# Attention with a gated MLP on one core: one tile of each unit's exponentials folded on GpSimd instead of VectorE

## The chip, the core and the metric

The kernel runs on one core of one Trainium2 chip. The metric is the device time of one execution in microseconds; before the change the median of three runs is 1235.76 us (1235.67 to 1236.98). The engines are TensorE (PE in the profile), VectorE (DVE), ScalarE (ACT), GpSimd (POOL) and SyncE (SP), which here only issues DMAs. Each engine works through its own instructions in order and waits for other engines by semaphores.

## The reference

`x` is the layer norm of `A_x` (2048 tokens, width 512). Attention has 32 heads of width 128 against a cache of 2048 keys; beside it runs an MLP with shifted columns, and its result gates the attention's.

```
xn = layernorm(A_x)
q = xn @ wq                                    # 32 heads x 128
p = softmax(q @ k_cache^T / sqrt(128))         # 2048 x 2048 per head
s = (p @ v_cache) @ wo
hs = shift(gelu(layernorm(xn) @ w1)) @ w2      # four column blocks, shifted by 1, -1, 2, -2 tokens
x1 = xn + hs
g = silu(x1 + gelu(layernorm(x1) @ w3) @ w4)
out = A_x + s * g
```

## The kernel before

The program has a prologue (layer norms and the MLP, up to about 118 us), one long attention loop, and a tail with the last unit in halves.

**Units and slots.** Attention is cut into 128 units: a unit is one head for 512 queries. The order is by groups of four heads (`NG` = 8 groups), in a group by block of queries (`QT` = 4), in that by head. A unit has eight slots (`SPU`); slot p computes the scores of 256 keys against 512 queries on TensorE (`s_slot`, two matmuls of 512 columns into one PSUM tile) and their exponentials on ScalarE (line 436), which go to a tile `pT` of 128 x 4 x 512 in bf16. Two slots fill one such tile, so a unit has four: slots 0 and 1, 2 and 3, 4 and 5 (the third tile), 6 and 7. The ring holds six. `pv_slot` multiplies them by the values ten slots later (`LAG`).

The loop over `n = u * SPU + p` writes out all engines' order by hand: `pin` keeps every instruction in the order in which the program issues it. So an instruction of VectorE that waits holds up everything that stands behind it on VectorE.

**The softmax sums.** VectorE adds the unit's four tiles: `add_first` (line 442, tiles 0 and 1, at slot 4), `add_next(u, 2)` (line 447, third tile, at slot 6), and in slot 0 of the next unit `add_next(u, 3)` (line 447, fourth tile). Then `fold` (line 451) adds the upper half of the 2048 columns to the lower, and `fold_last` (line 455) does it once more, which leaves 128 x 512. SyncE issues a transposing DMA of that (`turn`, line 480, slot 3). In slot 0 of the unit after, `turned_sums` (line 485) sums the transposed tile `tT`, `turned_recip` (line 491) inverts it, and two DMAs (`dr`, line 493, and `rb`, line 497) spread it over the partitions. At slot 7 `norm` (line 509) multiplies the unit's output `ps_o` by it.

So slot 0 of unit u holds on VectorE, in this order: the column sum and the reciprocal of unit u - 2, the last add of unit u - 1; then come, mixed with parts of the query product, the two folds of unit u - 1.

**The query products.** From unit 16 on, the query projection of two heads at a time is computed in seven smaller products (`product`, on block sums of `x` and of the weights), started two units ahead. TensorE writes them into one PSUM tile (tag `xa`); `q_take` (ScalarE, line 405) and `q_part` (VectorE, lines 413, 416, 418, 421) combine them into the queries. Lines 416 and 418 stand around the fold of an odd unit's slot 1; product 4, at slot 4 of the odd unit, writes where they read, and so waits for line 418. In the profile it is the matmul `ps_q<-xnT,wc`. The block sums of the weights are made by `w_sum` (line 365), four small subtractions for every pair of heads, two per unit, at slots 2 and 6 of two units.

**The output.** Each unit also has one tile of 128 tokens of the output projection (`wo_mm`, four matmuls into `ps_wo`), added to the sums `sacc` at slot 7 (`wo_post`, line 571). In the last groups the gate is applied: for the later two blocks of queries in group 6 by a product into a temporary `tm` and an add (lines 564 and 567); for the earlier two in group 7 by line 580, and the residual by line 582. `tm` has two buffers in the pool `pS`. Also for the later blocks lines 537 and 542 scale the sums and add the residual, once per unit, in some of the units before that.

GpSimd has work in the prologue alone: an iota, some memsets, and the powers of the layer norms (lines 194 and 205).

Of the kernel before, what the change touches and what calls it, by code (L numbers as in the profile page):

```python
# [9 lines left out]
ALU = mybir.AluOpType  # L10
FP32 = mybir.dt.float32
BF16 = mybir.dt.bfloat16
# [5 lines left out]
def kernel(  # L18
# [15 lines left out]
    nc = tc.nc  # L34
    P = nc.NUM_PARTITIONS
# [15 lines left out]
    HG = 4  # L51
    NG = H // HG

    SPU = KC // 2
# [7 lines left out]
    pin = tc.keep_in_program_order  # L62
# [48 lines left out]
    def mm(out, lhsT, rhs, start, stop, **kw):  # L111
# [9 lines left out]
        out=ident[:], in0=diag[:], scalar1=0.0, scalar2=None, op0=ALU.is_equal))  # L121
# [9 lines left out]
    kTs, vBs, wqs, wos, oTs, st = {}, {}, {}, {}, {}, {}  # L131
    todo = defaultdict(list)

    def at(n, fn):
        todo[n].append(fn)
# [179 lines left out]
    def q_mm(u, dcs, tag="xa"):  # L315
        g, qt, hh = units[u]
        if dcs[0] == 0:
            st[u] = dict(psq=psX.tile([P, 512], FP32, tag=tag, name="ps_q"))
        for dc in dcs:
            mm(st[u]["psq"][:], wqs[g * HG + hh][:, dc, :],  # L320
               xnT[:, dc, qt * 512:(qt + 1) * 512], dc == 0, dc == DC - 1)
# [37 lines left out]
    def w_sum(h, i):  # L359
        if i == 0:  # L360
            wc[h] = pS.tile([P, 4, 2, Dh], BF16, tag="wc", bufs=2, name="wc")
        w, o = wc[h], [wc[h][:, k] for k in range(4)]
        b11, b12, b21, b22 = (wqs[h + j][:, d, :] for d in (LO, HI) for j in (0, 1))
        a, b = ((b12, b11), (b22, o[0]), (b22, b12), (b21, o[1]))[i]
        pin(nc.vector.tensor_tensor(out=o[i], in0=a, in1=b, op=ALU.subtract))
# [59 lines left out]
    def s_slot(u, p):  # L425
        g, qt, hh = units[u]
        s = st[u]
        sps = psS.tile([P, 2, 512], FP32, name="ps_s")
        for j in range(2):
            kc = 2 * p + j  # L430
            kv = kTs[g * HG + hh].rearrange("d (i p j) -> d i j p", p=P, j=KJ)
            mm(sps[:, j, :], kv[:, kc // KJ, kc % KJ, :], s["qT"], True, True)
        if p % 2 == 0:
            s.setdefault("pT", []).append(pB.tile([P, 4, 512], BF16, tag="pT", bufs=6, name="pT"))
        jj = 2 * (p % 2)
        pin(nc.scalar.activation(  # L436
            out=s["pT"][-1][:, jj:jj + 2, :], in_=sps[:], func=ACT.Exp, scale=SCALE))

    def add_first(u):
        s = st[u]  # L440
        s["acc"] = pB.tile([P, 4, 512], BF16, tag="acc", bufs=2, name="acc")
        pin(nc.vector.tensor_tensor(  # L442
            out=s["acc"][:], in0=s["pT"][0][:], in1=s["pT"][1][:], op=ALU.add))

    def add_next(u, i):
        a = st[u]["acc"]
        pin(nc.vector.tensor_tensor(out=a[:], in0=a[:], in1=st[u]["pT"][i][:], op=ALU.add))  # L447

    def fold(u):
        a = st[u]["acc"]  # L450
        pin(nc.vector.tensor_tensor(out=a[:, 0:2, :], in0=a[:, 0:2, :], in1=a[:, 2:4, :], op=ALU.add))  # L451

    def fold_last(u):
        a = st[u]["acc"]
        pin(nc.vector.tensor_tensor(out=a[:, 0, :], in0=a[:, 0, :], in1=a[:, 1, :], op=ALU.add))  # L455
# [22 lines left out]
    def turn(u):  # L478
        st[u]["tT"] = pB.tile([P, 4, P], BF16, tag="tT", bufs=2, name="tT")
        pin(nc.sync.dma_start_transpose(out=st[u]["tT"][:], in_=st[u]["acc"][:, 0, :]))  # L480

    def turned_sums(u):
        s = st[u]
        sm = s["sm"] = smp.tile([P, 4], FP32, name="sm")
        pin(nc.vector.tensor_reduce(out=sm[:], in_=s["tT"][:], axis=mybir.AxisListType.X, op=ALU.add))  # L485

    def turned_recip(u):
        s = st[u]
        sm = s["sm"]
        rc = smp.tile([P, 4], FP32, name="rc")  # L490
        pin(nc.vector.reciprocal(out=rc[:], in_=sm[:]))
        s["dr"] = drp.tile([P, 4], FP32, name="dr")
        pin(nc.sync.dma_start(out=s["dr"][:], in_=rc[:]))

    def bcast(u):
        st[u]["rb"] = pB.tile([P, 512], FP32, tag="rb", bufs=2, name="rb")
        pin(nc.sync.dma_start(
            out=st[u]["rb"][:], in_=st[u]["dr"][:].rearrange("p j -> (p j)").partition_broadcast(P)))
# [52 lines left out]
    def pay():  # L551
        while owed:
            y_out(*owed.popleft(), nc.sync)
# [280 lines left out]
    pS = None  # L834
    for h in range(HG):
        load_wo(h)
    for g in range(NG - 1):
        b = (g * QT + QT - 1) * HG
        for hh in range(HG):
            h = (g + 1) * HG + hh  # L840
# [30 lines left out]
    def pv_run(n):  # L871
        while pv_at[0] <= n - LAG:
            pv_slot(*divmod(pv_at[0], SPU))
            pv_at[0] += 1
# [9 lines left out]
    UA, UB = NU - 2, NU - 1  # L884

    def wo_slot(part, n, each=2, **kw):
        gg, t = wo_todo[0]
        if part < HG // each:
            wo_mm(gg, t, tuple(range(part * each, (part + 1) * each)), **kw)
            return  # L890
        wo_todo.popleft()
        wo_post(gg, t, n)
        if gg == NG - 1 and t % 4 < 3 and t + 1 not in fin and t // 4 not in LATE:
            fin_load(t + 1)

    FIRST, LAST = 16, NU - 4
    pairs = range(FIRST, LAST + 1, 2)
    q_plan = defaultdict(list)
    steps = defaultdict(list)
    first, third = {}, {}  # L900
    for v in pairs:
        a = (v - 2) * SPU
# [8 lines left out]
    def fold_at(u):  # L911
        return 1 if u in third else 0

    def run_steps(n, which):
        for fn, v, k in steps.get(n, ()):
            if fn is which:
                fn(v, k)
# [4 lines left out]
    for h in range(HG, H, 2):  # L922
        u = (h // HG) * QT * HG + (-4, -2)[h % HG // 2]
        for i in range(4):
            at((u + i // 2) * SPU + (2, 6)[i % 2], lambda h=h, i=i: w_sum(h, i))

    for v in range(1, NU):
        if v not in made and not FIRST <= v < LAST + 2:
# [3 lines left out]
    for n in range(UB * SPU):  # L932
        u, p = divmod(n, SPU)
        extra = len(wo_todo) > 1 and u in (2 * HG, 2 * HG + 1)
        if p == 0 and wo_box:
            wo_slot(4, n, each=1)
        s_slot(u, p)
        pv_run(n)
        for v, dcs in q_plan.get(n, ()):
            q_mm(v, dcs)  # L940
        run_steps(n, product)
        run_steps(n, q_take)
        if p == 0 and 1 <= u:
            if u - 2 in TURN:
                turned_sums(u - 2)
                turned_recip(u - 2)
            add_next(u - 1, 3)
        if p == 1 and u - 2 in TURN:
            bcast(u - 2)
        if p == fold_at(u) and 1 <= u:  # L950
            for v in third.get(u, ()):
                q_part(v, 1)
            fold(u - 1)
            for v in third.get(u, ()):
                q_part(v, 2)
            if u != UA and u not in first:
                fold_last(u - 1)
        if p == 2 and u in first:
            q_part(first[u], 0)
            fold_last(u - 1)  # L960
        if p == 3 and u - 1 in TURN:
            turn(u - 1)
        if p == 0:
            twice = extra
        if twice and p < 3:
            wo_slot(p, n, tag="xa")
        for v, k in ((u + 1, 3), (u + 2, 7)):
            if p == k and "psq" in st.get(v, ()) and (k == 3) == (v > FIRST):
                q_copy(v)
        if u - 2 in TURN:  # L970
            norm_p, sum_p, wo_p, each = 7, 5, 3, 1
        else:
            norm_p, sum_p, wo_p, each = 4, 5, 4, 1
        at_wo = [wo_p + i for i in range(HG // each + 1)]
        if FIRST - 2 <= u < LAST:
            at_wo = ([1, 3, 4, 6, 7], [0, 2, 3, 6, 7])[u % 2]
        if p == norm_p and 2 <= u and not u - 2 in TURN:
            norm_queue(u - 2)
        if p == sum_p and 1 <= u and u - 1 not in TURN:
            sums(u - 1)  # L980
        if p == sum_p + 1 and 1 <= u and u - 1 not in TURN:
            bcast(u - 1)
        if u == UA and p in (1, 2, 3):
            wo_slot(p - 1, n)
            if p == 3:
                fold_last(u - 1)
        if p in at_wo and wo_todo and pS is not None and (p == at_wo[0] or wo_box):
            wo_slot(at_wo.index(p), n, each=each)
        if p == norm_p and u - 2 in TURN:
            norm_queue(u - 2)  # L990
        run_steps(n, q_part)
        if p == 4:
            add_first(u)
        if p == 6:
            add_next(u, 2)
        pay()
        held_mm(n)
        for fn in todo.pop(n, ()):
            fn()
        if pS is None and not held:  # L1000
            right.close()
            pS = right.enter_context(pool("pS", side="right", reuse_waits="tile"))
# [31 lines left out]
    def pv_to(k):  # L1034
# [29 lines left out]
        out=diag[:], in0=diag[:], scalar1=0.0, scalar2=None, op0=ALU.is_equal))  # L1064
# [98 lines left out]
```

## Time and profile before

| | |
|---|---|
| median of three runs | 1235.76 us (1235.67 to 1236.98) |
| the profiled execution | 1236.42 us |
| its span, first to last instruction | 1234.6 us |
| scores, values, output projection, queries in the loop | from about 118 to 1213 us |
| exponentials, line 436 | 1016 of 1025 ns |
| line 447 (third and fourth tile) | 254 of 1208 ns |
| line 442 (first two tiles) | 127 of 1224 ns |
| transposes of the sums to landing | 2.6 / 3.6 / 6.0 us (least, median, most) |

Engine names in the profile: PE is the matmul, PEld its weight loads, and SPq stands for what SyncE's queue issues. A timeline row gives the start in us, the duration in us, engine, line, operation, output and inputs, their shapes, a count, and in brackets how long the engine had been idle and what ended it. Consecutive instructions of VectorE overlap by some 0.09 us, so that their starts lie closer than their durations. A matmul of 512 columns shows 0.38 us, but they follow one another every 0.216 us. A group's row gives the count, the busy time in us and the mean in ns of one, and the engine's idle time before them. A row of the windows gives the length, then for PE, PEld, DVE, ACT and POOL the busy time and the number of instructions, the granted clock of TensorE, the DMA engines' share and GB/s.

### The profile page before, as it was taken

The page shows a single profiled execution, that of the slowest core. Times are in us where ns is not written, and L with a number is a line of the kernel's source. Part 1 is how long each engine was busy: PE and PEld are TensorE (multiplying, and loading weights), DVE is VectorE, ACT ScalarE, POOL GpSimd, SP SyncE. Part 2 cuts the span into 40 slices and gives each one's busy share as a digit, 9 for nine tenths or more (in the row PEclk, how much of TensorE's full clock was granted, in tenths as well). Part 3 has the DMA queues.
Part 4 walks back from the last instruction along what each step waited for, and adds up shares of the span by engine and source line. Part 5 has one row for each costly group of instructions (what it writes and reads, how often), then busy time and mean ns, then how long its engine had stood idle before and what let it go on. Part 6 is the DMA issues. An engine that isn't in the chain of part 4 may idle for free.

```text
span 1234.6 us, 17534 instructions
## 1 busy us (share of the span) xinstructions
PE 1227.5 (99%) x6267; PEld 636.5 (52%) x6267; DVE 1030.1 (83%) x1647; ACT 1105.8 (90%) x1237; POOL 26.6 (2%) x75
## 2 busy tenths in 40 slices
PE   9999999999999999999999999999999999999998
PEld 6444444455555555555555555555555555555545
DVE  7712778899888888988889888888889999999997
ACT  6345999899999999999999999999999999999996
POOL 5300000000000000000000000000000000000000
PEclk9999999999999999999999999999999999999999
DMA  8661122664334423354243523543345424553342
GB/s 176 168 140 35 31 39 65 96 99 94 63 80 100 106 57 82 87 111 85 58 95 91 111 56 69 103 104 72 76 83 111 107 58 90 99 107 66 77 81 66
DMA packets 244056, 107.75 MB, mean 87 GB/s; under 512 B 194816, under 2 KB 227712, under 8 KB 243968
## 3 DMA queue, kind: packets, MB, share of 16 engines
q1 hardware_dynamic: 243408, 106.17, 41.5%
q8 instruction: 49, 0.80, 0.3%
q10 hardware_dynamic: 560, 0.46, 0.1%
q14 instruction: 39, 0.32, 0.1%
HBM read 67.50 MB, written 2.36 MB: 57 GB/s over the span
## 4 chain that ended last, share of the span: by engine, by line
PE 94%; DVE 3%; DMA 2%; ACT 1%; issue 0%; SPq 0%; DVEq 0%; ACTq 0%
PE ps_s L112 39%; PE ps_o L112 37%; PE ps_wo L112 8%; PE ps_q L112 8%; PE ps_m L112 2%; DMA tT<-acc 1%; DVE acc L447 1%; ACT pT L436 1%; DMA rb<-dr 0%; DMA xin<-in_A_x_dram 0%; DVE sm L485 0%; PE ps_oh L112 0%; DVE oT L509 0%; DVE acc L451 0%; DVE y L1025 0%
## 5 line engine op out<-in xcount | busy, mean ns | idle before, releaser
L436 ACT ACTIVATE pT<-ps_s 128x1024 bf16<-128x1024 f32 x1016 | 1016.2, 1025 | 56.8 <-PE ps_s L112 26.1
L112 PE MATMUL ps_s<-qT,kT 128*128 128x512 bf16 (+1 forms) x2064 | 609.3, 378 | 0.0
L112 PE MATMUL ps_o<-pT,vb 128*128 128x512 bf16 x1984 | 590.2, 379 | 0.0
L447 DVE TENSOR_TENSOR acc<-acc,pT 128x2048 bf16<-128x2048 bf16 x254 | 307.0, 1208 | 54.9 <-ACT pT L436 54.4
L112 PEld LDWEIGHTS <-kT 128*128 128x128 bf16 x2064 | 232.7, 113 | 151.3 <-issue 1.0
L112 PEld LDWEIGHTS <-vb 128*128 128x128 bf16 x1984 | 193.9, 98 | 216.6
L442 DVE TENSOR_TENSOR acc<-pT 128x2048 bf16<-128x2048 bf16 x127 | 155.4, 1224 | 38.4 <-ACT pT L436 35.5
L112 PE MATMUL ps_wo<-wo_h,oT 128*128 128x512 bf16 x496 | 186.3, 379 | 0.0
L451 DVE TENSOR_TENSOR acc<-acc 128x1024 bf16<-128x1024 bf16 x127 | 87.4, 688 | 2.5
L509 DVE TENSOR_TENSOR oT<-ps_o,rb 128x512 bf16<-128x512 f32 x127 | 86.6, 682 | 1.1 <-DMA rb<-dr 0.8
L485 DVE TENSOR_REDUCE sm<-tT 128x4 f32<-128x512 bf16 x124 | 83.9, 676 | 2.8 <-DMA tT<-acc 2.7
L112 PEld LDWEIGHTS <-oT 128*128 128x128 bf16 x528 | 51.4, 98 | 52.6 <-issue 0.6
L112 PEld LDWEIGHTS <-wc 128*128 128x128 bf16 x440 | 43.0, 98 | 54.1 <-issue 2.7
L571 DVE TENSOR_TENSOR sacc<-ps_wo,sacc 128x512 f32<-128x512 f32 x96 | 65.7, 684 | 0.0
L112 PEld LDWEIGHTS <-wq_h 128*128 128x128 bf16 x398 | 38.9, 98 | 46.3
L112 PE MATMUL ps_q<-xnT,wq_h 128*128 128x256 bf16 (+1 forms) x288 | 61.1, 298 | 0.4 <-DVE sacc L559 0.4
L421 DVE TENSOR_TENSOR qT<-ps_q,tq 128x512 bf16<-128x512 f32 x55 | 38.0, 692 | 23.3 <-PE ps_q L112 22.9
L455 DVE TENSOR_TENSOR acc<-acc 128x512 bf16<-128x512 bf16 x127 | 52.9, 417 | 0.5
L293 ACT ACTIVATE h2T<-ps_s 128x1024 bf16<-128x1024 f32 x28 | 28.6, 1023 | 25.9 <-PE ps_s L112 25.9
L112 PE MATMUL ps_s<-xn2T,w_sb 128*128 128x512 bf16 x224 | 48.8, 379 | 0.0
L112 PEld LDWEIGHTS <-w_sb 128*128 128x128 bf16 x368 | 33.5, 98 | 29.6
L112 PE MATMUL ps_q<-xs,wc 128*128 128x256 bf16 x246 | 47.0, 273 | 0.0
(102 smaller groups left out, 585.6 us busy)
## 6 DMA issues: line engine op xcount, KB each, us to landing
rb<-dr SPq DMA_DIRECT2D x127, 256.0 KB, 3.9
vb<-in_A_v_cache_dram SPq DMA_DIRECT2D x62, 256.0 KB, 3.0
wq_h<-in_A_wq_dram SPq DMA_DIRECT2D x32, 128.0 KB, 3.0
wo_h<-in_A_wo_dram SPq DMA_DIRECT2D x32, 128.0 KB, 2.5
w_sb<-in_B_w_dram SPq DMA_DIRECT2D x8, 256.0 KB, 5.0
kT<-in_A_k_cache_dram SPq DMA_TRANSPOSE x128, 2.8
xl<-in_A_x_dram SPq DMA_DIRECT2D x16, 128.0 KB, 3.0
dr<-rc SPq DMA_DIRECT2D x127, 2.0 KB, 1.4
```

What stands on the lines that cost most here:

```text
L112: pin(nc.tensor.matmul(out=out, lhsT=lhsT, rhs=rhs, start=start, stop=stop, **kw))
L293: pin(nc.scalar.activation(out=h2[c, f][:], in_=ps[:], func=ACT.Gelu_apprx_tanh))
L421: pin(nc.vector.tensor_tensor(out=s["q"][:, 1:3], in0=ps, in1=u.to_broadcast([P, 2] + list(u.shape[2:])), op=ALU.add))
L436: pin(nc.scalar.activation(out=s["pT"][-1][:, jj:jj + 2, :], in_=sps[:], func=ACT.Exp, scale=SCALE))
L442: pin(nc.vector.tensor_tensor(out=s["acc"][:], in0=s["pT"][0][:], in1=s["pT"][1][:], op=ALU.add))
L447: pin(nc.vector.tensor_tensor(out=a[:], in0=a[:], in1=st[u]["pT"][i][:], op=ALU.add))
L451: pin(nc.vector.tensor_tensor(out=a[:, 0:2, :], in0=a[:, 0:2, :], in1=a[:, 2:4, :], op=ALU.add))
L455: pin(nc.vector.tensor_tensor(out=a[:, 0, :], in0=a[:, 0, :], in1=a[:, 1, :], op=ALU.add))
L485: pin(nc.vector.tensor_reduce(out=sm[:], in_=s["tT"][:], axis=mybir.AxisListType.X, op=ALU.add))
L509: pin(nc.vector.tensor_tensor(out=to, in0=o, in1=rb, op=ALU.mult))
L571: pin(nc.vector.tensor_tensor(out=sa, in0=ps[:], in1=sa, op=ALU.add))
```

## The change

For units 24 to 124 (`APART`) the third tile isn't added whole by VectorE any more. At slot 6, where that add stood, GpSimd adds the tile's upper half to its lower half into a tile `ph` of 128 x 2 x 512 (`add_aside`). In slot 0 of the next unit, between the reciprocal and the last add, VectorE adds `ph` to the lower half of the accumulator (`add_join`); the later folds then sum the same numbers. `ph` shares the two buffers of `tm`. Besides, the second and fourth of the weights' block sums are issued at slot 4 instead of slot 6, for all pairs of heads. The instructions of TensorE and ScalarE and the DMAs keep their number and order.

```diff
+    def add_aside(u):
+        s = st[u]
+        s["ph"] = pS.tile([P, 2, 512], BF16, tag="tm", bufs=2, name="ph")
+        pin(nc.gpsimd.tensor_tensor(
+            out=s["ph"][:], in0=s["pT"][2][:, 0:2, :], in1=s["pT"][2][:, 2:4, :], op=ALU.add))
+
+    def add_join(u):
+        a = st[u]["acc"]
+        pin(nc.vector.tensor_tensor(
+            out=a[:, 0:2, :], in0=a[:, 0:2, :], in1=st[u].pop("ph")[:], op=ALU.add))
...
     FIRST, LAST = 16, NU - 4
+    APART = range(FIRST + 2 * HG, UA - 1)
...
-            at((u + i // 2) * SPU + (2, 6)[i % 2], lambda h=h, i=i: w_sum(h, i))
+            at((u + i // 2) * SPU + (2, 4)[i % 2], lambda h=h, i=i: w_sum(h, i))
...
             if u - 2 in TURN:
                 turned_sums(u - 2)
                 turned_recip(u - 2)
+            if u - 1 in APART:
+                add_join(u - 1)
             add_next(u - 1, 3)
...
         if p == 6:
-            add_next(u, 2)
+            add_aside(u) if u in APART else add_next(u, 2)
```

## The prediction

> **What bounds the kernel now.** I read the page first (busy time, the chain that ended last), then the sums by window, then what TensorE waited for, and last the timeline of one unit pair in the middle and of two near the end.
>
> ```profile
> span 1234.6 us, 17534 instructions
> PE 1227.5 (99%) x6267; PEld 636.5 (52%) x6267; DVE 1030.1 (83%) x1647; ACT 1105.8 (90%) x1237; POOL 26.6 (2%) x75
> POOL 5300000000000000000000000000000000000000
> PE 94%; DVE 3%; DMA 2%; ACT 1%; issue 0%; SPq 0%; DVEq 0%; ACTq 0%
> ...
> 400.00:500.00 100.00, 100.00 (x505) 52.08 (x504) 86.05 (x132) 95.76 (x107) 0.00 (x0) 1.00 0.37 80
> 1050.00:1100.00 50.00, 49.02 (x249) 25.55 (x248) 46.48 (x78) 46.77 (x53) 0.00 (x0) 1.00 0.50 102
> 1150.00:1195.00 45.00, 44.55 (x221) 22.67 (x220) 43.40 (x66) 42.41 (x47) 0.00 (x0) 1.00 0.41 77
> ...
> PE ps_q L112 <- DVE qT L418: 1.4, 3, 1.0
> ```
>
> TensorE is the bound: 94% of the chain is its own, and between 400 and 500 us it is busy for all of the window (second column) at a granted clock of 1.00. There VectorE (fourth column, 86.05) has 14 us to spare, so shortening VectorE by itself buys nothing there. Only near the end does TensorE stand still inside the loop: 0.98 us in the 1050 window, 0.45 in the 1150 window, and 0.16 at 1011.89 (row below): 1.6 us in all, and what it waited for three times is line 418, the VectorE add that frees the query product's accumulator. GpSimd has done nothing since the prologue, so its queue is empty when the new instruction comes.
>
> What decides is therefore how far line 418 lies ahead of the TensorE product that needs it. In the middle:
>
> ```profile
> 609.69 1.20 SPq L480 DMA_TRANSPOSE tT<-acc  x1
> ...
> 612.16 1.23 DVE L447 TENSOR_TENSOR acc<-acc,pT 128x2048 bf16<-128x2048 bf16 x1 [0.93 <-ACT pT L436]
> 612.42 0.38 PE L112 MATMUL ps_wo<-wo_h,oT 128*128 128x512 bf16 x1
> 613.30 0.68 DVE L571 TENSOR_TENSOR sacc<-ps_wo,sacc 128x512 f32<-128x512 f32 x1
> 614.50 0.68 DVE L485 TENSOR_REDUCE sm<-tT 128x4 f32<-128x512 bf16 x1
> 615.22 0.18 DVE L491 RECIPROCAL rc<-sm 128x4 f32<-128x4 f32 x1
> 615.31 1.20 DVE L447 TENSOR_TENSOR acc<-acc,pT 128x2048 bf16<-128x2048 bf16 x1
> 617.35 0.42 DVE L418 TENSOR_TENSOR qT<-ps_q,tq 128x256 bf16<-128x256 f32 x1
> 618.90 0.38 PE L112 MATMUL ps_q<-xnT,wc 128*128 128x256 bf16 x2
> ...
> DMA to landing us min/median/max: 2.6/3.6/6.0
> ```
>
> Line 418 ends at 617.77, TensorE comes to its product at 618.90: 1.13 us of slack. From 612.16 to 617.77 VectorE works without a pause, so whatever is added there eats this slack.
>
> **The change part by part.** Its prices come from these rows:
>
> ```profile
> L447 DVE TENSOR_TENSOR acc<-acc,pT 128x2048 bf16<-128x2048 bf16 x254 | 307.0, 1208 | 54.9 <-ACT pT L436 54.4
> L451 DVE TENSOR_TENSOR acc<-acc 128x1024 bf16<-128x1024 bf16 x127 | 87.4, 688 | 2.5
> L365 DVE TENSOR_TENSOR wc<-wq_h 128x256 bf16<-128x256 bf16 x28 | 8.0, 285 | 0.0
> L567 DVE TENSOR_TENSOR sacc<-sacc,tm 128x512 f32<-128x512 f32 x8 | 5.5, 692 | 0.3
> L580 DVE SCALAR_TENSOR_TENSOR xall<-sacc,xall 128x512 bf16<-128x512 f32 x8 | 5.5, 692 | 0.3
> L194 POOL TENSOR_TENSOR rs<-ve,nhalf 128x1 f32<-128x1 f32 x32 | 18.3, 573 | 5.8 <-DVE ve L205 3.3
> L205 POOL TENSOR_SCALAR ve<-mv 128x1 f32<-128x1 f32 x30 | 8.0, 267 | 21.2 <-DVE mv L203 21.2
> L118 POOL IOTA diag<- 128x128 f32 x1 | 0.2, 242 | 0.4 <-POOLq L1147 0.4
> ```
>
> 1. *VectorE's add of the third tile goes* in 101 units (24 to 124): 1208 ns each. It stood behind a wait of 0.93 us for ScalarE, and the next instruction needs the output projection's last matmul, which ends at 612.42 + 0.38 = 612.80. So line 571 starts at 612.80 rather than 613.30: only 0.50 us of the 1.2 become an advance. Is the column sum (line 485) then held by its transpose? Issued at 609.69, with the median 3.6 us it lands at 613.3, before the new 614.00. No.
>
> 2. *The join comes*, 688 ns like line 451 of the same shape, between the reciprocal and the last add. That add reads what the join wrote; such dependent neighbours start 0.72 apart (614.50 to 615.22 for the reduce and its reciprocal), so 0.72 is the price. Net for line 418: -0.50 + 0.72 = +0.22 us, out of 1.13: 0.91 are left. In the middle this costs nothing, the cover being that slack. VectorE's load falls by 1208 - 688 = 520 ns a unit, which is off the path.
>
> 3. *GpSimd's fold* of 128x1024 with two inputs is shown by no row. Lower bound: VectorE's 0.69. Upper: the iota writes 128 elements in 242 ns; eight times that is 1.94 us for one stream, and twice that, 3.87, if its two inputs are read one after the other. I take 1.94 plus what a second operand adds on the same engine for one element (573 - 267 ns): 2.24 us, nearest to the only rows of that engine. It starts when the tile's second half is written (612.16) and ends at 614.40. The join can start at 614.72 + 0.09 = 614.81, so up to 2.65 us of fold it doesn't wait; a fold over 2.65 + 0.91 = 3.56 would stall TensorE in every pair. What stands behind the join on VectorE is all of the chain to line 418, the last fold and the transpose that SP issues after it; their waiter is the product at 618.90.
>
> The Trainium skill (GPSIMD Engine Reference, Performance versus the Vector engine) gives 4497 ns for a GpSimd add of 2048 fp32 elements per partition; half of it, an estimate, would be 2.25 us, and the sum by it would stay as it is.
>
> 4. *VectorE and GpSimd at once.* From the fold's start to its end VectorE runs lines 571, 509 and 485 in the middle, each with one input from PSUM or a single input. Near the end there stand also lines 567 (8 units) and 580 with 582 (8 units), all operands in SBUF. What does GpSimd reading SBUF do to these? In the prologue a GpSimd power that otherwise takes 573 ns took 740 beside VectorE's SBUF-to-SBUF work:
>
> ```profile
> 52.79 2.64 DVE L219 TENSOR_SCALAR xn<-xall,mv,rs 128x512 bf16<-128x512 bf16 x8
> 52.79 0.74 POOL L194 TENSOR_TENSOR rs<-ve,nhalf 128x1 f32<-128x1 f32 x1
> ...
> 1091.63 1.23 DVE L447 TENSOR_TENSOR acc<-acc,pT 128x2048 bf16<-128x2048 bf16 x1 [0.43 <-ACT pT L436]
> 1091.89 0.38 PE L112 MATMUL ps_wo<-wo_h,oT 128*128 128x512 bf16 x1
> 1093.49 0.69 DVE L567 TENSOR_TENSOR sacc<-sacc,tm 128x512 f32<-128x512 f32 x1
> 1097.55 0.42 DVE L418 TENSOR_TENSOR qT<-ps_q,tq 128x256 bf16<-128x256 f32 x1
> 1098.37 0.38 PE L112 MATMUL ps_q<-xnT,wc 128*128 128x256 bf16 x2
> ...
> 1142.84 1.23 DVE L447 TENSOR_TENSOR acc<-acc,pT 128x2048 bf16<-128x2048 bf16 x1 [0.63 <-ACT pT L436]
> 1143.09 0.38 PE L112 MATMUL ps_wo<-wo_h,oT 128*128 128x512 bf16 x1
> 1144.70 0.69 DVE L580 SCALAR_TENSOR_TENSOR xall<-sacc,xall 128x512 bf16<-128x512 f32 x1
> 1149.22 0.42 DVE L418 TENSOR_TENSOR qT<-ps_q,tq 128x256 bf16<-128x256 f32 x1
> 1149.69 0.38 PE L112 MATMUL ps_q<-xnT,wc 128*128 128x256 bf16 x2
> ```
>
> So the two engines can hold each other up. For a long fold the bounds are no hold and a hold to the fold's end; I take the full hold, as the one row of the two together shows one. Unit at 1142.84: the fold ends at 1145.08. Line 580 could start 0.51 early, at 1144.19, but starts at 1145.08, 0.38 late; with the join line 418 is 1.10 late, and its slack (1149.64 to 1149.69) is 0.05: TensorE loses 1.05. The L567 units: the matmul ends at 1092.27, lines 564 and 567 could start there and 0.71 on, the fold ends at 1093.87, 0.38 after 1093.49; again 1.10, against a slack of 0.40 (1097.97 to 1098.37): 0.70. Line 418 runs in every second unit, and the last two L580 units lie past unit 124, so there are 4 pairs of the one and 3 of the other: 4 x 0.70 + 3 x 1.05 = 6.0 us.
>
> The Trainium skill (SBUF — State Buffer, Who interferes with whom) says that a VectorE instruction with two SBUF inputs and a GpSimd instruction that reads SBUF exclude each other, the later one waiting for the whole of the earlier. By that rule the 6.0 us are certain; no run here shows it for such a pair.
>
> 5. *Stalls on the transpose.* Where the column sum waits for its transpose, nothing is gained by step 1 and the join's 0.72 counts whole:
>
> ```profile
> 1007.96 0.69 DVE L485 TENSOR_REDUCE sm<-tT 128x4 f32<-128x512 bf16 x1 [0.70 <-DMA tT<-acc]
> ...
> 1011.89 0.38 PE L112 MATMUL ps_q<-xnT,wc 128*128 128x256 bf16 x2 [0.16 <-DVE qT L418]
> ```
>
> There are two such places (this one and the 1050 window); 0 to 1.4 us, I take 0.7, because the transpose may itself land earlier or later.
>
> 6. *The weights' block sums* move from slot 6 to slot 4: half of the 56 instructions (28 of 285 ns), on VectorE alone, no DMA with them. They leave the busy stretch behind the third tile's add for the wait of 0.93 us in front of it; nothing, or 28 x 0.2 us of VectorE's time without that cover, which the slack takes. They read weights loaded units before. The fold's result shares two buffers with tm: the order fold, tm, join lets each be free in time, nothing. The exponential tile is read until 614.40 rather than 613.39, but TensorE reads it ten slots later anyway: nothing.
>
> Sum: 6.0 + 0.7 = 6.7 us on the profiled execution's 1236.4 us (its span of 1234.6 and 1.8 around it), 1243.1. The median of the three runs, 1235.8, lies 0.66 lower, so I predict 1242.4.
>
> **The rivals.** *No hold*: the engines run side by side. Then line 418 comes 0.22 later; the three pairs without slack pay 0.2 each and step 5 its 0.7: +1.3, 1237.1. For it: nothing in the middle is touched. Against: the 0.74 row. *A gain*: with 0.52 us less VectorE work per unit the late stalls vanish; at most the 1.6 us that TensorE stood still: 1234.2. For it: VectorE is 46.5 of 50 busy there. Against: the join lies behind the waits, the removed add in front of them. *A long fold*: from 3.56 us on, the join itself becomes the wait in all pairs. At the upper bound of 3.87: 0.31 in each of 35 pairs before 925 us (11 us), (3.87 - 2.65 + 0.22 - 0.40) in each of some 8 pairs to 1065 (8), and 1.63 more in each of the 7 late pairs (11), on top of 6.7: 37 us, 1272. For it: the join is VectorE's first wait for GpSimd in the loop. Against: my estimate lies 1.3 below. That the fold doesn't run beside VectorE at all can't be: its queue is empty and its tile ready.
>
> **How the numbers follow.** Hold 0.50, no hold 0.25, long fold 0.17, gain 0.08. A difference under 0.2% (2.5 us) counts as none: the no-hold case falls there, half of the gain, the hold seldom; so faster 0.04, same 0.29, slower 0.67. The hold's own range: fold 1.9 to 3.2 us, +4 to +15, 1240 to 1250. The whole range reaches down over the no-hold case and most of the gain to 1234.6, and up into folds just over 3.3 us, to 1252; about 0.05 lies below and 0.13 above.
>
> **What would show it.** The fold's mean near 2.2 us, and no wait of the join for it in the middle; lines 571 half a microsecond earlier; TensorE full between 400 and 900 us; gaps before line 567's and 580's successors that end with the fold, and TensorE waiting some 1 us for line 418 in each pair from 1076 to 1187 us. I am wrong if these two lines start with the fold still running, or if the join waits for GpSimd in the middle.

## The result and the profile after

The changed kernel takes 1244.68 us (median of six runs, 1244.02 to 1245.38) against 1235.72 us before: a ratio of 1.0071, with a 95% interval of 1.0061 to 1.0081, or some 9 us more. Line numbers after the change are higher by 11 to 14: the accumulate add 447 is 458, the column sum 485 is 496, line 567 is 578, 571 is 582, 580 is 591, 582 is 593; the new fold on GpSimd is line 448 and the join 453. Lines 413 to 436 and 442 stay.

From the page of the kernel after, the span, the busy times and the chain that ended last, and from the list of waits the one row of TensorE for line 418:

```profile
span 1243.2 us, 17616 instructions
PE 1223.4 (98%) x6149; PEld 637.8 (51%) x6267; DVE 1001.3 (81%) x1647; ACT 1106.7 (89%) x1237; POOL 242.7 (20%) x176
PE 87%; DVE 9%; DMA 2%; issue 1%; ACT 1%; DVEq 0%; ACTq 0%
...
PE ps_q L112 <- DVE qT L418: 7.7, 9, 1.5
```

VectorE's busy time has fallen by 29 us, and yet it holds three times as much of the chain (9% instead of 3%). TensorE now waits nine times for line 418 rather than three. (This trace has records of 6149 of the 6267 matmuls, so TensorE's busy time and share are shown a little low.) The groups of the kernel after say where VectorE's time went:

```profile
L448 POOL TENSOR_TENSOR ph<-pT 128x1024 bf16<-128x1024 bf16 x101 | 216.1, 2140 | 934.1 <-ACT pT L436 927.8 <-DVE acc L442 6.3
L453 DVE TENSOR_TENSOR acc<-acc,ph 128x1024 bf16<-128x1024 bf16 x101 | 66.7, 661 | 0.0
L582 DVE TENSOR_TENSOR sacc<-ps_wo,sacc 128x512 f32<-128x512 f32 x96 | 66.4, 692 | 81.1 <-PE ps_wo L112 59.2 <-PE ps_s L112 21.7
L578 DVE TENSOR_TENSOR sacc<-sacc,tm 128x512 f32<-128x512 f32 x8 | 11.0, 1370 | 0.3
L591 DVE SCALAR_TENSOR_TENSOR xall<-sacc,xall 128x512 bf16<-128x512 f32 x8 | 11.3, 1414 | 0.3
```

The fold takes 2.14 us and the join never waits for it (0.0 us of idle time before line 453). Line 582, with one input from PSUM, runs beside the fold in 692 ns (684 before). Lines 578 and 591, each with two inputs in SBUF, have doubled from 692 ns to 1370 and 1414.

The timeline in the middle, at the place that was shown of before, and then of a late unit:

```profile
612.28 2.13 POOL L448 TENSOR_TENSOR ph<-pT 128x1024 bf16<-128x1024 bf16 x1 [6.30 <-ACT pT L436]
612.91 0.69 DVE L582 TENSOR_TENSOR sacc<-ps_wo,sacc 128x512 f32<-128x512 f32 x1 [1.60 <-PE ps_wo L112]
614.12 0.68 DVE L496 TENSOR_REDUCE sm<-tT 128x4 f32<-128x512 bf16 x1
614.92 0.66 DVE L453 TENSOR_TENSOR acc<-acc,ph 128x1024 bf16<-128x1024 bf16 x1
615.69 1.23 DVE L458 TENSOR_TENSOR acc<-acc,pT 128x2048 bf16<-128x2048 bf16 x1
617.77 0.42 DVE L418 TENSOR_TENSOR qT<-ps_q,tq 128x256 bf16<-128x256 f32 x1
618.98 0.38 PE L112 MATMUL ps_q<-xnT,wc 128*128 128x256 bf16 x2
...
1147.02 2.13 POOL L448 TENSOR_TENSOR ph<-pT 128x1024 bf16<-128x1024 bf16 x1 [6.30 <-ACT pT L436]
1148.32 1.38 DVE L591 SCALAR_TENSOR_TENSOR xall<-sacc,xall 128x512 bf16<-128x512 f32 x1
1154.32 0.42 DVE L418 TENSOR_TENSOR qT<-ps_q,tq 128x256 bf16<-128x256 f32 x1
1154.79 0.38 PE L112 MATMUL ps_q<-xnT,wc 128*128 128x256 bf16 x2 [0.97 <-DVE qT L418]
```

In the middle line 418 ends at 618.19 and TensorE comes at 618.98: 0.79 us of the former 1.13 are left, and nothing is lost. The column sum, line 496, begins before the fold's end (614.41) and takes 0.68 us as before: its single input lies in SBUF too, and it isn't held. Late, line 591 begins 1.30 us into the fold, the fold ends at 1149.15, and line 591 ends at 1149.70. Alone it takes 0.69 us, and 0.55 of them come after the fold's end: nearly all of it has waited until the fold was over. Everything behind it is late, and TensorE waits.

How much TensorE loses is read from the distance between its starts, less the usual distance (0.216 us after a matmul of 512 columns), because the bracket starts only after the 0.38 us with which the matmul before is shown. In front of the product that waits for line 418 this makes, in us:

| place | before | after |
|---|---|---|
| 1011.9 | 0.32 | 0.22 |
| 1046 | 0 | 0.36 |
| 1064 | 1.14 | 1.63 |
| four pairs with line 578 (1082 to 1137) | 0 | 0.61, 0.67, 0.94, 1.05 |
| three pairs with line 591 (1154 to 1192) | 0.12, 0.45, 0.11 | 1.13, 1.40, 1.39 |
| sum | 2.1 | 9.4 |

That is 7.3 of the 8.6 us by which the span grew. Another 0.8 is lost at the end, which the timeline there shows:

```profile
1201.37 1.22 DVE L442 TENSOR_TENSOR acc<-pT 128x2048 bf16<-128x2048 bf16 x1
1201.93 2.64 POOL L448 TENSOR_TENSOR ph<-pT 128x1024 bf16<-128x1024 bf16 x1 [5.98 <-ACT pT L436]
...
1203.28 1.84 DVE L591 SCALAR_TENSOR_TENSOR xall<-sacc,xall 128x512 bf16<-128x512 f32 x1
...
1210.00 0.68 DVE L331 CAST qT<-ps_q 128x512 bf16<-128x512 f32 x1
1210.74 0.27 PE L112 MATMUL ps_sum<-ones_t,acc 128*128 128x1 bf16 x4 [0.67 <-DVE qT L331]
```

Unit 124 is the last with a fold, and in it one more line 591 is held. VectorE doesn't catch up in the seven microseconds to line 331, for which TensorE's next product waits.

### The profile page after: what moved, and what is told of

It is laid out like the page before. It is cut to its first block, busy times and chain, and to the rows that moved or that the text cites. A ratio compares the mean times of both kernels' runs of the same rounds, so it can differ in the third digit from the quotient of the medians.

```text
span 1243.2 us, 17616 instructions
## 1 busy us (share of the span) xinstructions
PE 1223.4 (98%) x6149; PEld 637.8 (51%) x6267; DVE 1001.3 (81%) x1647; ACT 1106.7 (89%) x1237; POOL 242.7 (20%) x176
## 4 chain that ended last, share of the span: by engine, by line
PE 87%; DVE 9%; DMA 2%; issue 1%; ACT 1%; DVEq 0%; ACTq 0%
PE ps_s L112 36%; PE ps_o L112 33%; PE ps_q L112 8%; PE ps_wo L112 7%; PE ps_m L112 2%; DVE acc L458 2%; DMA tT<-acc 1%; DVE sm L496 1%; ACT pT L436 1%; DVE acc L453 1%; DVE acc L462 1%; DVE oT L520 1%; DVE xall L591 1%; DMA rb<-dr 0%; DVE sacc L582 0%
## 5 line engine op out<-in xcount | busy, mean ns | idle before, releaser
L112 PE MATMUL ps_o<-pT,vb 128*128 128x512 bf16 x1906 | 573.0, 379 | 3.3
L448 POOL TENSOR_TENSOR ph<-pT 128x1024 bf16<-128x1024 bf16 x101 | 216.1, 2140 | 934.1 <-ACT pT L436 927.8
L458 DVE TENSOR_TENSOR acc<-acc,pT 128x2048 bf16<-128x2048 bf16 x153 | 186.8, 1221 | 25.2 <-ACT pT L436 13.4
L112 PE MATMUL ps_wo<-wo_h,oT 128*128 128x512 bf16 x475 | 178.4, 379 | 0.0
L453 DVE TENSOR_TENSOR acc<-acc,ph 128x1024 bf16<-128x1024 bf16 x101 | 66.7, 661 | 0.0
```

The source lines that it names most:

```text
L112: pin(nc.tensor.matmul(out=out, lhsT=lhsT, rhs=rhs, start=start, stop=stop, **kw))
L448: pin(nc.gpsimd.tensor_tensor(out=s["ph"][:], in0=s["pT"][2][:, 0:2, :], in1=s["pT"][2][:, 2:4, :], op=ALU.add))
```

## The experiments

Two theories were set against each other. *Hold*: the time goes to lines 578 and 591, which stand still while GpSimd folds. *Join*: it goes to the join's 0.7 us between the reciprocal and the last add, or to the buffers shared with `tm`. All ratios are to the kernel before on the same chip, with 95% intervals.

### The fold by VectorE

```diff
     def add_aside(u):
-        pin(nc.gpsimd.tensor_tensor(
+        pin(nc.vector.tensor_tensor(
```

> The fold of the third tile is done by VectorE at the same place; join, order and buffers stay as in the change. Theory (hold): what costs the time is VectorE waiting for GpSimd's fold in lines 578 and 591. Without GpSimd both are back at 0.69 us and line 418 is only some 0.2 us late, so 1236 to 1238 us. Rival (join): the time goes to the join's 0.7 us behind the reciprocal and to the shared buffers; both are still there, so 1243 to 1245 us.

1238.96 us, ratio 1.0024 (1.0014 to 1.0033). A row of its groups, and one pair of its timeline:

```profile
L578 DVE TENSOR_TENSOR sacc<-sacc,tm 128x512 f32<-128x512 f32 x8 | 5.5, 692 | 0.3
...
1150.98 0.42 DVE L418 TENSOR_TENSOR qT<-ps_q,tq 128x256 bf16<-128x256 f32 x1
1151.45 0.38 PE L112 MATMUL ps_q<-xnT,wc 128*128 128x256 bf16 x2 [0.29 <-DVE qT L418]
```

Line 578 is back at 692 ns with the join and the shared buffers in place, and so is line 591. Two thirds of the loss are gone (0.71% to 0.24%), as the hold has it; by the join theory all of it should have stayed. The 3 us that stay are a little more than the 0 to 2 expected. TensorE loses 4.1 us at its waits (by the distances between starts) instead of 2.1, at 1012, 1047, 1065 and some of the late pairs. VectorE here carries the fold's 0.69 us and the join in place of one add of 1.2, which is the likely cause; no run separates the two.

### The fold and the join only in units 24 to 109

```diff
-    APART = range(FIRST + 2 * HG, UA - 1)
+    APART = range(FIRST + 2 * HG, 110)
```

> The fold and the join only in units 24 to 109, before the first unit with line 578. Hold: the 6.5 us of TensorE waits in the late pairs and the 0.8 at the end go, the 0.7 of the two places where the column sum waits for its transpose stays: 1236 to 1237 us. A rival by which the 86 early units cost something of their own (fold and join in the middle): half or more of the 9 us stays, 1240 us or more.

1237.53 us, ratio 1.0012 (1.0003 to 1.0021). TensorE's wait in its list:

```profile
PE ps_q L112 <- DVE qT L418: 1.7, 4, 0.7
```

So 86 units with a fold cost some 1.5 us together (0.4 to 2.6), and the 15 units of the end the remaining 7: the loss sits where lines 578 and 591 are. By itself this doesn't tell the hold from the join, since those units have lost their join too. The median lies half a microsecond above what was expected; the interval, 1236.3 to 1238.5 us, reaches into it.

### A longer fold

```diff
         pin(nc.gpsimd.tensor_tensor(
             out=s["ph"][:], in0=s["pT"][2][:, 0:2, :], in1=s["pT"][2][:, 2:4, :], op=ALU.add))
+        pin(nc.gpsimd.tensor_tensor(
+            out=s["ph"][:, 0, :], in0=s["ph"][:, 0, :], in1=s["ph"][:, 1, :], op=ALU.add))
...
-            out=a[:, 0:2, :], in0=a[:, 0:2, :], in1=st[u].pop("ph")[:], op=ALU.add))
+            out=a[:, 0, :], in0=a[:, 0, :], in1=st[u].pop("ph")[:, 0, :], op=ALU.add))
```

> GpSimd folds the third tile twice, to 512 columns, in two instructions, and the join is 512 wide. Hold: GpSimd is at work some 1.1 us longer (half of 2.14), so the 7 late pairs lose some 1.1 us more each, less the 0.27 us that the join is shorter: 5 to 7 us above the change, 1250 to 1252 us; line 578 takes about 2.4 us. In the middle the join may wait some 0.7 us for GpSimd, inside the slack of 0.9. Join theory: the join is 0.27 us shorter, so 7 x 0.27 = 2 us below the change, 1242 to 1243 us.

1249.42 us, ratio 1.0109 (1.0096 to 1.0123): 4.7 us above the change, a little under the 5 to 7 expected, though the join is shorter. But the groups don't show the 2.4 us that I expected of the first held line (the last row is of TensorE's waits):

```profile
L450 POOL TENSOR_TENSOR ph<-ph 128x512 bf16<-128x512 bf16 x101 | 121.7, 1205 | 7.9
L455 DVE TENSOR_TENSOR acc<-acc,ph 128x512 bf16<-128x512 bf16 x101 | 42.4, 420 | 54.8 <-POOL ph L450 54.8
L580 DVE TENSOR_TENSOR sacc<-sacc,tm 128x512 f32<-128x512 f32 x8 | 10.7, 1333 | 0.3
L595 DVE TENSOR_TENSOR xl<-xall,xl 128x512 bf16<-128x512 bf16 x8 | 9.2, 1155 | 0.3
...
PE ps_o L112 <- DVE oT L522: 4.3, 7, 1.0
```

Line 580 (here what 578 was) takes 1333 ns, much as with the single fold, and the line after the gate, 595, goes from 424 ns to 1155. The hold lasts for one GpSimd instruction: between the two VectorE gets in, and the second instruction then holds the next line.

So the time isn't lost where I expected it. By the distances between starts the seven late pairs lose less at line 418 than with the single fold, 5.5 us for 7.2. In its place TensorE's product with the values waits seven times for line 522, the `norm` (509 before), which stands behind the held line 595. The second fold also makes the join wait, 54.8 us in 101 units. Until some 940 us that stays inside the slack. From 943 to 1049 us seven pairs, in which no line is held, lose 2.8 us together where the change loses 0.6, so a part of the 4.7 us is the join's wait and not the hold.

### The block sums at slot 6

```diff
-            at((u + i // 2) * SPU + (2, 4)[i % 2], lambda h=h, i=i: w_sum(h, i))
+            at((u + i // 2) * SPU + (2, 6)[i % 2], lambda h=h, i=i: w_sum(h, i))
```

> The change with the weights' block sums left at slots 2 and 6. Hold: the one at slot 6 of an odd unit (line 365, both inputs in SBUF) comes when the fold has just begun and takes some 2.2 us instead of 0.28; the one of an even unit is through before the fold begins. The delay falls on the half of the pair that has slack, so the time is 0 to 2 us above the change. No hold: line 365 stays at 0.28 us and the time is that of the change.

1256.67 us, ratio 1.0164 (1.0149 to 1.018): 12 us above the change, where 0 to 2 were expected. The line is held as foreseen, but not in every second unit only: of the 28 in the group below 18 are held, three at a time in neighbouring units. Its group, the row of a new wait of TensorE, and two units of the timeline:

```profile
L365 DVE TENSOR_TENSOR wc<-wq_h,wc 128x256 bf16<-128x256 bf16 x28 | 41.3, 1477 | 0.0
...
PE ps_wo L112 <- DVE sacc L582: 3.7, 5, 0.7
...
382.02 2.12 POOL L448 TENSOR_TENSOR ph<-pT 128x1024 bf16<-128x1024 bf16 x1 [6.52 <-ACT pT L436]
382.18 2.11 DVE L365 TENSOR_TENSOR wc<-wq_h,wc 128x256 bf16<-128x256 bf16 x1
...
389.72 1.22 DVE L442 TENSOR_TENSOR acc<-pT 128x2048 bf16<-128x2048 bf16 x1
390.45 2.47 POOL L448 TENSOR_TENSOR ph<-pT 128x1024 bf16<-128x1024 bf16 x1 [6.30 <-ACT pT L436]
390.85 2.21 DVE L365 TENSOR_TENSOR wc<-wq_h,wc 128x256 bf16<-128x256 bf16 x1
392.99 0.68 DVE L582 TENSOR_TENSOR sacc<-ps_wo,sacc 128x512 f32<-128x512 f32 x1
```

At 382.18 the small subtraction stands 2.11 us instead of 0.28. VectorE is then so late that in the next unit its add 442 still runs when the fold begins, and the subtraction behind it, which was expected to be through by then, falls into the fold as well. The second delay comes on top of the first, and five times even the output projection waits for line 582. The miss was to take the next unit's order of events from a timeline in which VectorE is on time.

### Only the move of the block sums

The same line in the kernel before, the other way round, and nothing else:

```diff
-            at((u + i // 2) * SPU + (2, 6)[i % 2], lambda h=h, i=i: w_sum(h, i))
+            at((u + i // 2) * SPU + (2, 4)[i % 2], lambda h=h, i=i: w_sum(h, i))
```

> Only the move of the weights' block sums to slot 4, on the kernel before. Both theories: within 0.5 us of the kernel before (1235.2 to 1236.2 us).

1235.64 us, ratio 0.9998 (0.9989 to 1.0006): nothing, as expected.

### The late lines behind the join

Lines 578 (567 before the change) and 591 with 593 are issued four slots later, at slot 3 of the next unit:

```diff
-                pin(nc.vector.tensor_tensor(out=sa, in0=sa, in1=tm[:], op=ALU.add))
+                at(n + 4, lambda: pin(nc.vector.tensor_tensor(out=sa, in0=sa, in1=tm[:], op=ALU.add)))
...
+        def finish():
...
+        if n + 4 < UB * SPU:
+            at(n + 4, finish)
+        else:
+            finish()
```

with lines 591, 593 and the output's DMA in `finish`. Once on the change, once on the kernel before:

> The change, with lines 578, 591 and 593 (and the output's DMA) issued four slots later, at slot 3 of the next unit, when GpSimd is idle. Hold: they are back at 0.69 us, line 418 of the late pairs is no longer late; the waits of 1.6 and 0.4 us at two earlier places remain: 1235 to 1237 us. Join theory: the join still stands in front of line 418, 1241 us or more.

1236.61 us, ratio 1.0005 (0.9996 to 1.0014). All 101 folds are still on GpSimd and all 101 joins in place. The group and the wait in this kernel:

```profile
L578 DVE TENSOR_TENSOR sacc<-sacc,tm 128x512 f32<-128x512 f32 x8 | 5.5, 685 | 0.0
...
PE ps_q L112 <- DVE qT L418: 1.7, 3, 1.2
```

> The same deferral on the kernel before, without GpSimd. The three waits of TensorE on line 418 after 1149 us (0.12, 0.45 and 0.11) go, the others stay: 0.3 to 1.2 us below the kernel before, 1234.5 to 1235.5 us. If the deferral itself is what makes the deferred form of the change fast, it gains here as much as there (8 us), which TensorE's 1.6 us of idle time in the loop rules out.

1235.27 us, ratio 0.9994 (0.9985 to 1.0003), in the range that was expected, but not told apart from no gain. The deferral takes 8 us from the change and under 1 from the kernel before. It does two things at once: it removes the meeting with the fold, and it takes 0.7 us (line 578) or 1.1 us (lines 591 and 593) of work away from in front of line 418, room into which the join fits. The kernel before can't show the worth of that room, because it has only 0.7 us to lose at those places. So this pair of runs alone doesn't tell hold from join; the fold by VectorE does, where both the late lines and the join stay and 5.7 of the 9 us go.

### Room in front of line 418

The same two, with lines 537 and 542 (scaling the sums, adding the residual) moved from slot 0 to slot 3, and the block sums at slot 4 in both:

```diff
-        k = n + SPU * (t - 4 * LATE[0]) + 1
+        k = n + SPU * (t - 4 * LATE[0]) + 4
```

> The kernel before without GpSimd, with the deferral of lines 567, 580 and 582, the block sums at slot 4, and lines 537 and 542 moved from slot 0 to slot 3. Both theories: line 418 gets its slack back in all pairs, TensorE no longer waits for it, 1.6 to 2.5 us below the kernel before: 1233.4 to 1234.6 us.

1234.46 us, ratio 0.9977 (0.9967 to 0.9986). The kernel before takes 1237.33 us on this chip, so the gain is 2.9 us, a little over the 1.6 to 2.5 expected. TensorE's list of waits has none for line 418.

> The same moves on the change, so that GpSimd's fold stays in 101 units and no line with both inputs in SBUF stands beside it. Hold: no wait of TensorE on line 418 is left, and as TensorE is the bound the fold brings nothing: within 0.7 us of the same moves without GpSimd, 1233.4 to 1235.2 us. Join theory: at least 2 us slower than the same moves without GpSimd. If VectorE's 52 us less of work did count, it would be faster than those by more than 0.7 us.

1234.94 us, ratio 0.9981 (0.9972 to 0.9990). The windows of 1050 to 1100 us, first without GpSimd and then with it (columns as before: length, TensorE, its weight loads, VectorE, ScalarE, GpSimd), and TensorE's wait for line 418 with it:

```profile
1050.00:1100.00 50.00, 50.00 (x253) 26.03 (x252) 46.78 (x79) 47.65 (x54) 0.00 (x0) 1.00 0.47 99
...
1050.00:1100.00 50.00, 49.43 (x251) 25.71 (x249) 44.56 (x78) 47.08 (x54) 11.44 (x7) 1.00 0.54 100
PE ps_q L112 <- DVE qT L418: 0.6, 1, 0.6
```

Both beat the kernel before by some 0.2%. The fold on GpSimd takes 2.2 us of VectorE's work out of this window and brings nothing: the medians differ by 0.5 us, the wrong way for it, and the two intervals overlap. Where no wait was expected, one of 0.57 us is left with the fold, and it is as large as the difference. Otherwise TensorE has no wait for line 418 left in the loop.

## Why the prediction was right

1. *VectorE's add goes.* Right. Line 582 starts 0.63 us after the third tile is ready (612.91 after 612.28), where 0.64 was worked out, and waits for the matmul; the rest of the 1.2 us is idle time (1.60 in its bracket, with the 0.93 of before).
2. *The join.* 661 ns rather than 688, but the add behind it starts 0.77 after it, not 0.72. The slack that is left in the middle is 0.79, where 0.91 was expected; it costs nothing there, as said.
3. *The fold.* 2.14 us, for an estimate of 2.24. It was put together from an iota and a power, instructions of another kind, so that it came so near is partly luck. The join doesn't wait, so the long fold falls as a rival. The estimate of 2.25 us worked out from the Trainium skill's page (GPSIMD Engine Reference, Performance versus the Vector engine) is as near.
4. *The hold.* Taken as full, and it nearly was (0.55 of 0.69 us behind the fold's end). TensorE's loss in the four pairs and the three is 6.5 us (3.3, and 3.9 less the 0.7 of before) for 6.0 predicted; the join's 0.72 is in both. The fold by VectorE takes the hold away and leaves the join. The units up to 109 alone lose the late joins as well, and the deferred lines make room for the join, so these two agree with the hold without proving it. The sign of being wrong was badly put: lines 578 and 591 do start with the fold still running, because the profile counts the held time inside the instruction (1370 and 1414 ns for 692), and there is no gap behind them. By its words that sign was met; the durations are what shows the hold. The rule of the Trainium skill (SBUF — State Buffer, Who interferes with whom) holds in this trace: 1370 ns beside the fold, 692 without it, and 692 also beside it for line 582, which has one input from PSUM.
5. *The transposes.* 0.7 taken; the first three places of the table lose 2.21 instead of 1.46, so 0.75. That the sum fits is luck: of the two places named, that at 1011.9 loses 0.1 less than before and that at 1064 0.5 more, and one at 1046 that wasn't named adds 0.4.
6. *The block sums.* Moving them costs nothing, as priced. What the prediction didn't ask is what the move spares: without it the change would cost 12 us more.

The sum was 6.7 us and the span grew by 8.6. Nearly half of what is missing is a hold left out. Step 4 says that the last two units with line 580 lie past unit 124; in fact only the last one does. So line 591 of unit 124 was held too, and the tail paid 0.8 for it. The rest is 0.5 too little in step 4 and some 0.5 whose place stays open.

Of the rivals, *no hold* fell with lines 578 and 591. Its price of 1.3 us has no run of its own: the fold by VectorE, the nearest, cost 3 us (1.7 to 4.1), but there VectorE does the fold itself. *A gain* fell too: even where every wait for line 418 but one is gone, GpSimd's help is worth nothing.

## What to carry to other kernels

Here work that was taken from an engine that isn't the bound bought nothing, and where its replacement met other work it cost time. Before moving an add to GpSimd, list what VectorE runs from the add's start to its end. In these runs instructions with two inputs in SBUF stood still for that time (692 ns became 1370); those with one of two inputs from PSUM (line 582, 692 ns) or with a single input (line 496, 676 ns) didn't. And look for the units that differ from the one in the middle: of the 9 us, 86 of the 101 units cost some 1.5 and the other 15 the rest.

## What the hardware showed

The hold works in both directions: the fold at 1201.93 took 2.64 us instead of 2.13, where VectorE's add 442, with two inputs in SBUF, was still at work for 0.66 us when it started. It lasts for one instruction: with the fold in two (2.14 and 1.2 us), VectorE's held line (1333 ns) ran between them, and the next was held by the second, 1155 ns instead of 424. And it accumulates: a subtraction of 0.28 us that met the fold in one unit pushed that of the next unit into it, and a part that was expected to cost 0 to 2 us cost 12.
